# Sliding dilated attention beside a gated FFN: one quadrant run and one Exp for each block's logits, sums of four products everywhere, and a new order of TensorE's work

## The chip, the cores and the metric

The kernel runs on one core of one Trainium2 chip. Its time is device microseconds (us) of one execution; a lower number is better. All runs that are compared were fast (TensorE's clock granted at 0.99 or more of full speed).

## The reference, cut to what matters

```python
def _A_ref(x, wqkv, wo):                 # attention: 32 heads of 16, window 8, dilation 2
    H = 32; Dh = D // H
    W, dil = 8, 2
    qkv = ...(x @ wqkv)...
    idx = pos[:, None] - (jnp.arange(W) * dil)[None, :]
    mask = idx >= 0
    kg = k[:, :, idx_c, :]; vg = v[:, :, idx_c, :]
    logits = jnp.einsum("bhsd,bhswd->bhsw", q, kg) * scale
    attn = _softmax(jnp.where(mask, logits, -1e9), axis=-1)
    o = jnp.einsum("bhsw,bhswd->bhsd", attn, vg)
    return o @ wo                        # s

def _B_ref(x, w_gate, w_up, w_down):     # FFN, 512 -> 1792 -> 512
    h = _gelu(x @ w_gate) * (x @ w_up)
    return h @ w_down                    # y

xn = _layernorm(x)                       # x is 2048 x 512, bf16
return x + _A_ref(xn, ...) * _silu(_B_ref(xn, ...))
```

## The kernel before

The 2048 tokens are worked on in four blocks of 512 (`j` = 0 to 3). For each block TensorE computes QKV; VectorE multiplies q by eight shifted views of k and adds products; TensorE sums what is left over the 16 channels of a head with a "quadrant" matmul, in which 128 rows become 32, so that four of them lie side by side in one PSUM tile (L, the logits); ACT takes the Exp. The window's sums (`sum_ps`), their reciprocals spread back (`b_ps`) and the products with v (`pv`, reduced to O by another quadrant run) follow in the same way. The FFN runs as 14 pairs of g (gate) and u (up) for each block, each four matmuls of 128x512, and y is 14 matmuls for each tile of 128 tokens.

The whole program is a list of tasks. A small list scheduler orders them at build time, by the durations and priorities in the dictionary `G` and by rings of buffers; the instructions are then issued in that fixed order on each engine. `FULL`, `UPACT` and `TRACT` (transposed tiles that ACT copies) say which work is done and by which engine, and `fb`, `ab` and the like are the sizes of the rings; the rest of `G` sets the order and nothing else.

```python
G = dict(
    ... FULL=(2, 3), UPACT=tuple((j, fc) for j in (1, 2, 3) for fc in range(14)),
    BETWEEN={1: 4, 2: 3}, ... fb=4, ab=2, ob=1, prb=6, ...
)
# PSUM: four buffers "f" (qkv, g, u, y, s), two "a" (tr, L, sum, b), one double "O", each 128 x 512 f32

def scores(j, prio):
    full = j in G["FULL"]                       # sums of four products, or of two
    for w2 in range(2):                         # two halves of the window
        ...                                     # 4 products on VectorE, added in pairs; if full, the pairs too
        def reduce(w2=w2, prods=prods):
            L = psa.tile([P, TQ], F32, name="L_ps", tag="a")
            for i in range(1 if full else 2):
                for w4 in range(4):
                    nc.tensor.matmul(L[32 * w4 : 32 * (w4 + 1), :], lhsT=quad[:],
                        rhs=prods[2 * i][:, w4, :], start=(i == 0), stop=(i == 1 or full))
        def expo(w2=w2):
            nc.scalar.activation(out=attn[:, w2, :], in_=tiles["L", j, w2][:], func=AF.Exp)
    ...                                         # sums, recip, spread_back, b_copy
def ffn_pair(j, fc):
    copied_up = (j, fc) in G["UPACT"]           # ACT copies u to SBUF, or VectorE reads it in PSUM
    ...
def out_tile(j, tt, split):
    ...
    if tt == 0:
        s = add_s()
        y = add_y()
    else:
        y = add_y()
        s = add_s()
```

The softmax here doesn't subtract the row's maximum and nothing guards it: scores larger than these inputs give would overflow.

Of the kernel before, what the change touches and what calls it, by code (L numbers as in the profile page):

```python
# [9 lines left out]
ALU = mybir.AluOpType  # L10
# [4 lines left out]
P = 128  # L15
# [10 lines left out]
    MM=0.217, COL8=0.3, COL4=0.2, TR=0.354, PROD=1.167, HMUL=0.582, HMUL2=0.34, STATS=0.881,  # L26
    NORM=0.326, TRCOPY=0.444, ACT1=0.58, ACT2=1.087, TABLE=1.075, HOP=0.136, LOOK=0.275, vst=2.654,
    vload=3.833, vissue=2.706, TRACT=(), x2=13.724, x3=17.04, FULL=(2, 3), UPACT=tuple((j, fc) for j in (1, 2, 3) for fc in range(14)),
    BETWEEN={1: 4, 2: 3}, trig=[0, 0, 3, 3],
    s_prio=[1.0, 2.0, 3.5, 4.0], v_prio=[1.5, 2.0, 3.75, 4.5], e_lat=0.1, b_lat=0.1, p_sum=-1.5,  # L30
    p_red=-0.5, p_tr=-1.0, p_h=-1.4, wo_at=0, wd_at=1, fb=4, ab=2, ob=1, prb=6, vab=2, x_early=[3.2,
    3.5, 3.8, 4.1],
# [5 lines left out]
HMUL = G["HMUL"]  # L38
# [99 lines left out]
def kernel(  # L138
# [23 lines left out]
    def pool(name, bufs, **kw):  # L162
# [9 lines left out]
    prpool = pool("prpool", G["prb"])  # L172
    atpool = pool("atpool", 2)
# [12 lines left out]
        {"xn": 4, "q": 3, "vst": 4, "va": G["vab"], "pr": G["prb"], "attn": 2, "o": 2, "h0": 1, "h1": 1, "gl": 3, "sg": 3,  # L186
# [124 lines left out]
    def layer_norm(j):  # L311
# [38 lines left out]
        def transpose(t, dep, on_act):  # L350
# [17 lines left out]
            a = add("pe", TR, fn, deps=[dep], prio=G["p_tr"], takes=[("a", ("tr", t))], frees=[("xn", t)])  # L368
# [5 lines left out]
        if j == 0:  # L374

            behind = []
            for half in range(2):
                pair = list(ts)[2 * half : 2 * half + 2]
                for t, s in [(t, stat(t, behind)) for t in pair]:
                    transpose(t, norm(t, rstd_act(t, 1, [s])), on_act=t % 2 == 0)  # L380
                behind = [copied[t] for t in pair if t % 2 == 1]
        else:
            for half in range(2):
                pair = list(ts)[2 * half : 2 * half + 2]
                r = rstd_act(pair[0], 2, [stat(t) for t in pair])
                for t in pair:
                    transpose(t, norm(t, r), on_act=(j, half) in G["TRACT"])
# [24 lines left out]
    def qkv(j):  # L412
# [4 lines left out]
        for lo in range(0, TQ, n):  # L417
            for which in range(3):
                for c in range(0, NC, w):
# [47 lines left out]
                    if which == 0 and c == 0 and lo == 0:  # L467
                        takes = [("q", j)]
                    e = add(
                        "act", ACT1, evacuate, deps=[m], prio=-0.5, takes=takes,  # L470
# [45 lines left out]
    def scores(j, prio):  # L516
        exps = []
        full = j in G["FULL"]
        for w2 in range(2):
            prods = []  # L520

            def product(c, w2=w2, prods=prods):
                prod = prpool.tile([P, 4, TQ], BF16, name="prod", tag="pr")
                off = j * TQ + PAD - HALO + 8 * w2
                base = k_sb[:, c, off : off + TQ]
                kwin = bass.AP(
                    tensor=base.tensor, offset=base.offset, ap=[base.ap[0], [2, 4], [1, TQ]]
                )
                nc.vector.tensor_tensor(  # L529
                    out=prod[:],  # L530
                    in0=tiles["q", j][:, c, :].unsqueeze(1).to_broadcast([P, 4, TQ]),
                    in1=kwin,
                    op=ALU.mult,
                )
                prods.append(prod)

            def pair(i, prods=prods):
                a, b = prods[2 * i], prods[2 * i + 1]
                nc.vector.tensor_tensor(out=a[:], in0=a[:], in1=b[:], op=ALU.add)  # L539

            def reduce(w2=w2, prods=prods):
                L = psa.tile([P, TQ], F32, name="L_ps", tag="a")
                tiles["L", j, w2] = L
                for i in range(1 if full else 2):
                    for w4 in range(4):
                        nc.tensor.matmul(  # L546
                            L[32 * w4 : 32 * (w4 + 1), :],
                            lhsT=quad[:],
                            rhs=prods[2 * i][:, w4, :],
                            start=(i == 0),  # L550
                            stop=(i == 1 or full),
                        )

            def expo(w2=w2):
                if w2 == 0:
                    tiles["attn", j] = atpool.tile([P, 2, TQ], BF16, name="attn", tag="attn")
                attn = tiles["attn", j]
                nc.scalar.activation(out=attn[:, w2, :], in_=tiles["L", j, w2][:], func=AF.Exp)

            def masked(w2=w2):  # L560
                a = tiles["attn", j][:, w2, 0:PAD]
                nc.vector.tensor_tensor(out=a, in0=a, in1=mask[:, w2, :], op=ALU.mult)

            ps = []
            key = ("S", j, w2)
            for c in range(NC):
                last = c == NC - 1
                ps.append(
                    add(
                        "dve", PROD, lambda c=c, product=product: product(c),  # L570
                        deps=[q_ready[j], k_ready[j], *ps[-1:]], prio=prio,
                        takes=[("pr", (*key, c))], opens=key,
                        frees=[("q", j)] if w2 == 1 and last else [],
                    )
                )
                if c % 2 == 1:
                    ps.append(
                        add(
                            "dve", PROD, lambda c=c, pair=pair: pair(c // 2), deps=[ps[-1]], prio=prio,
                            opens=key, closes=key if last and not full else None,  # L580
                            frees=[("pr", (*key, c))],
                        )
                    )

            def whole(prods=prods):
                a, b = prods[0], prods[2]
                nc.vector.tensor_tensor(out=a[:], in0=a[:], in1=b[:], op=ALU.add)

            if full:
                ps.append(  # L590
                    add(
                        "dve", PROD, whole, deps=[ps[-1]], prio=prio, opens=key, closes=key,
                        frees=[("pr", (*key, 2))],
                    )
                )
            r = add(
                "pe", G["COL4"] if full else COL8, reduce, deps=[ps[-1]], prio=G["p_red"],
                takes=[("a", ("L", j, w2))], frees=[("pr", (*key, c)) for c in ((0,) if full else (0, 2))],
            )
            e = add(  # L600
                "act", ACT1, expo, deps=[r], prio=-0.6, func="exp",
                takes=[("attn", j)] if w2 == 0 else [], frees=[("a", ("L", j, w2))],
            )
            if j == 0:
                e = add("dve", 0.1, masked, deps=[e], prio=-1.5)
            exps.append(e)
# [41 lines left out]
    def values(j, prio):  # L648
# [10 lines left out]
        for half in range(2):  # L659
            pvs = []  # L660

            def product(g, w2, half=half, pvs=pvs):
                pv = prpool.tile([P, 4, TQ], BF16, name="pv", tag="pr")
                nc.vector.tensor_tensor(  # L664
                    out=pv[:],
                    in0=tiles["attn", j][:, w2, :].unsqueeze(1).to_broadcast([P, 4, TQ]),
                    in1=tiles["va", j, half][:, 4 * (g % 2) : 4 * (g % 2 + 1), 8 * w2 : 8 * w2 + TQ],
                    op=ALU.mult,
                )
                pvs.append(pv)  # L670

            def pair(gg, pvs=pvs):
                a, b = pvs[2 * gg], pvs[2 * gg + 1]
                nc.vector.tensor_tensor(out=a[:], in0=a[:], in1=b[:], op=ALU.add)  # L674

            def reduce(half=half, pvs=pvs):
                o_ps = pso.tile([P, 2, TQ], F32, name="O_ps", tag="o")
                tiles["O", j, half] = o_ps
                for gg in range(2):
                    for e in range(4):  # L680
                        nc.tensor.matmul(  # L681
                            o_ps[32 * e : 32 * (e + 1), gg, :],
                            lhsT=fold4[:, 0, :],
                            rhs=pvs[2 * gg][:, e, :],
# [12 lines left out]
            ps = []  # L697
            key = ("V", j, half)
            for i in range(4):
                last = i == 3  # L700
                ps.append(
                    add(
                        "dve", PROD,
                        lambda i=i, half=half, product=product: product(2 * half + i // 2, i % 2),
                        deps=[n, v_ready[j, half], *ps[-1:]], prio=prio,
                        takes=[("pr", (*key, i))], opens=key,
                        frees=([("va", (j, half))] if last else [])
                        + ([("attn", j)] if last and half == 1 else []),
                    )
                )  # L710
                if i % 2 == 1:
                    ps.append(
                        add(
                            "dve", PROD, lambda i=i, pair=pair: pair(i // 2), deps=[ps[-1]], prio=prio,
# [222 lines left out]
    for j in range(NJ):  # L937
        ffn_pairs(j, NF)
        for tt in range(TPB):
            out_tile(j, tt, j == NJ - 1 and tt == TPB - 1)  # L940
# [31 lines left out]
```

## Time and profile before

| kernel before | |
|---|---|
| time, median of 6 runs | 228.25 us (228.23 to 228.44) |
| span in the profile | 226.5 us |
| TensorE: first QKV matmul, end of the last s | 7.29, 222.85 us |
| quadrant runs for L | 8 (4 of eight matmuls, 4 of four) |
| table loads on ACT | 19 |

The prediction shows the lines themselves and reads them. One word is used throughout: the pitch is the distance between the starts of successive matmuls, 0.216 us for 128x512 here, so a wait of TensorE shows as a start that comes later than the pitch.

### The profile page before, as it was taken

The page shows a single profiled execution, that of the slowest core. Times are in us where ns is not written, and L with a number is a line of the kernel's source. Part 1 is how long each engine was busy: PE and PEld are TensorE (multiplying, and loading weights), DVE is VectorE, ACT ScalarE, POOL GpSimd, SP SyncE. Part 2 cuts the span into 40 slices and gives each one's busy share as a digit, 9 for nine tenths or more (in the row PEclk, how much of TensorE's full clock was granted, in tenths as well). Part 3 has the DMA queues.
Part 4 walks back from the last instruction along what each step waited for, and adds up shares of the span by engine and source line. Part 5 has one row for each costly group of instructions (what it writes and reads, how often), then busy time and mean ns, then how long its engine had stood idle before and what let it go on. Part 6 is the DMA issues. An engine that isn't in the chain of part 4 may idle for free.

```text
span 226.5 us, 3294 instructions
## 1 busy us (share of the span) xinstructions
PE 220.3 (97%) x1230; PEld 106.1 (47%) x1230; DVE 187.9 (83%) x278; ACT 137.4 (61%) x215; POOL 14.8 (7%) x46
## 2 busy tenths in 40 slices
PE   6999999999999999999999999999999999999993
PEld 2897544534544444444444444444444444444462
DVE  4899999999999999899999999999936999322232
ACT  3566675658777346297777435877772187767210
POOL 7100400000022000002100000202000000000000
PEclk9999999999999999999999999999999999999999
DMA  6994990293199500106280010267100100000001
GB/s 205 340 372 155 216 252 4 56 348 110 50 353 273 120 0 23 46 26 143 47 188 0 3 46 26 75 141 163 25 0 26 46 23 0 0 3 0 23 25 46
DMA packets 19216, 22.64 MB, mean 100 GB/s; under 512 B 1392, under 2 KB 18176, under 8 KB 19200
## 3 DMA queue, kind: packets, MB, share of 16 engines
q1 hardware_dynamic: 12832, 11.67, 18.7%
q10 hardware_dynamic: 5056, 6.49, 8.8%
q0 software_dynamic: 1312, 4.28, 8.1%
q8 instruction: 9, 0.15, 0.3%
q14 instruction: 7, 0.06, 0.1%
HBM read 18.22 MB, written 4.21 MB: 99 GB/s over the span
## 4 chain that ended last, share of the span: by engine, by line
PE 95%; DVE 2%; DMA 1%; issue 0%; DVEq 0%
PE y_ps L808 22%; PE g_ps L735 22%; PE u_ps L735 22%; PE qkv_ps L432 19%; PE s_ps L796 6%; PE O_ps L681 2%; PE tr_ps L354 2%; PE L_ps L546 2%; DMA x_sb<-in_A_x_dram 1%; DVE stats L318 1%; PE sum_ps L613 0%; PE b_ps L631 0%; DVE sg L825 0%; DVE xn_t L339 0%; DVE xnT L366 0%
## 5 line engine op out<-in xcount | busy, mean ns | idle before, releaser
L735 PE MATMUL g_ps<-xnT,wg_sb 128*128 128x512 bf16 x224 | 57.5, 379 | 0.0
L735 PE MATMUL u_ps<-xnT,wu_sb 128*128 128x512 bf16 x224 | 57.5, 379 | 0.0
L808 PE MATMUL y_ps<-wd_sb,hT 128*128 128x512 bf16 (+1 forms) x238 | 51.4, 367 | 0.0
L432 PE MATMUL qkv_ps<-xnT,wqkv_sb 128*128 128x512 bf16 (+1 forms) x240 | 43.6, 337 | 0.3 <-DVE xnT L366 0.3
L745 ACT ACTIVATE gl<-g_ps 128x512 bf16<-128x512 f32 x56 | 33.5, 598 | 16.9 <-PE g_ps L735 16.7
L664 DVE TENSOR_TENSOR pv<-attn,v_arr 128x2048 bf16<-128x2048 bf16 x32 | 38.5, 1219 | 0.1
L529 DVE TENSOR_TENSOR prod<-q_sb,k_sb 128x2048 bf16<-128x2048 bf16 x32 | 38.4, 1218 | 0.0
L808 PEld LDWEIGHTS <-hT 128*128 128x128 bf16 x238 | 22.7, 98 | 24.6 <-issue 0.9
L735 PEld LDWEIGHTS <-wu_sb 128*128 128x128 bf16 x224 | 21.5, 98 | 27.1 <-issue 2.1
L735 PEld LDWEIGHTS <-wg_sb 128*128 128x128 bf16 x224 | 21.5, 98 | 26.8 <-issue 1.5
L432 PEld LDWEIGHTS <-wqkv_sb 128*128 128x128 bf16 x240 | 25.0, 108 | 15.9 <-issue 1.8
L820 ACT ACTIVATE sil<-y_ps 128x512 bf16<-128x512 f32 (+1 forms) x17 | 9.7, 572 | 34.8 <-PE y_ps L808 34.8
L758 ACT ACTIVATE hT<-u_ps 128x512 bf16<-128x512 f32 x42 | 25.1, 598 | 8.8 <-PE u_ps L735 8.5
L763 DVE TENSOR_TENSOR hT<-gl,hT 128x512 bf16<-128x512 bf16 x42 | 17.6, 422 | 11.9 <-ACT hT L758 11.8
L825 DVE TENSOR_TENSOR sg<-sil,s_ps 128x512 bf16<-128x512 bf16 (+1 forms) x17 | 11.1, 653 | 12.2 <-PE s_ps L796 8.2
L674 DVE TENSOR_TENSOR pv<-pv 128x2048 bf16<-128x2048 bf16 x16 | 19.5, 1222 | 0.3
L539 DVE TENSOR_TENSOR prod<-prod 128x2048 bf16<-128x2048 bf16 x16 | 19.5, 1222 | 0.3
L504 POOL DMA_DIRECT2D v_arr<-vT_dram x16 | 9.3, 586 | 138.8 <-DVE pv L664 122.9
L796 PE MATMUL s_ps<-wo_sb,o_sb 128*128 128x512 bf16 (+1 forms) x68 | 16.4, 367 | 0.0
L451 ACT ACTIVATE k_sb<-qkv_ps 128x512 bf16<-128x512 f32 x16 | 9.4, 597 | 5.8 <-PE qkv_ps L432 5.8
L318 DVE BATCH_NORM_STATS2 stats<-x_sb 128x6 f32<-128x512 bf16 x16 | 10.8, 675 | 2.3 <-DMA x_sb<-in_A_x_dram 2.3
L445 ACT ACTIVATE q_sb<-qkv_ps 128x512 bf16<-128x512 f32 x16 | 9.5, 597 | 3.4 <-PE qkv_ps L432 3.1
(56 smaller groups left out, 141.2 us busy)
## 6 DMA issues: line engine op xcount, KB each, us to landing
v_arr<-vT_dram SPq DMA_DIRECT2D x16, 260.0 KB, 5.4
v_arr<-vT_dram POOLq DMA_DIRECT2D x16, 260.0 KB, 6.1
vT_dram<-vst SPq DMA_DIRECT2D x16, 128.0 KB, 4.4
out_dram<-sg SPq DMA_DIRECT2D x15, 128.0 KB, 1.7
wg_sb<-in_B_w_gate_dram ACTq DMA_DIRECT2D x2, 896.0 KB, 5.8
wu_sb<-in_B_w_up_dram ACTq DMA_DIRECT2D x2, 896.0 KB, 8.5
wd_sb<-in_B_w_down_dram ACTq DMA_DIRECT2D x1, 1792.0 KB, 9.0
wqkv_sb<-in_A_wqkv_dram SPq DMA_DIRECT2D x2, 512.0 KB, 6.0
```

Source lines behind the costliest of these rows:

```text
L318: nc.vector.bn_stats(out=stats[:, t, :], in_=x_sb[:, t, :])
L432: nc.tensor.matmul(ps[:, i * n : (i + 1) * n], lhsT=wqkv_sb[:, which, ws], rhs=xnT[:, dk, j * TQ + lo : j * TQ + lo + n], start=(dk == 0), ...
L529: nc.vector.tensor_tensor(out=prod[:], in0=tiles["q", j][:, c, :].unsqueeze(1).to_broadcast([P, 4, TQ]), in1=kwin, op=ALU.mult,)
L539: nc.vector.tensor_tensor(out=a[:], in0=a[:], in1=b[:], op=ALU.add)
L664: nc.vector.tensor_tensor(out=pv[:], in0=tiles["attn", j][:, w2, :].unsqueeze(1).to_broadcast([P, 4, TQ]), in1=tiles["va", j, half][:, 4 * ...
L674: nc.vector.tensor_tensor(out=a[:], in0=a[:], in1=b[:], op=ALU.add)
L735: nc.tensor.matmul(ps[:], lhsT=w[:, dk, fc * P : (fc + 1) * P], rhs=xnT[:, dk, j * TQ : (j + 1) * TQ], start=(dk == 0), stop=(dk == NC - 1),)
L745: nc.scalar.activation(out=tiles["gl", j, fc][:], in_=tiles["g_ps", j, fc][:], func=AF.Gelu_apprx_tanh)
L758: nc.scalar.activation(out=hidden(), in_=tiles["u_ps", j, fc][:], func=AF.Copy)
L763: nc.vector.tensor_tensor(out=h, in0=tiles["gl", j, fc][:], in1=u, op=ALU.mult)
L796: nc.tensor.matmul(tiles["s", t, cs.start][:], lhsT=tiles["o", j][:, c, tt * P : (tt + 1) * P], rhs=wo_sb[:, c, cs], start=(c == 0), stop= ...
L808: nc.tensor.matmul(tiles["y", t, cs.start][:], lhsT=tiles["h", j, fc // (NF // 2)][:, fc % (NF // 2), tt * P : (tt + 1) * P], rhs=wd_sb[:, ...
```

## The change

Its intent: make L in one run of eight matmuls on a double PSUM tile, with one 1024-wide Exp, where there were two runs and two Exps. To keep that run at eight matmuls in every block, VectorE adds four products everywhere (`FULL`), which costs it work in blocks 0 and 1. For that it is relieved elsewhere: ACT copies u in block 0 too, and eight transposed tiles. Six pairs stand between the QKV of blocks 1 and 2 (before: four there, and three between blocks 2 and 3), and y of a block's first two tiles goes by halves of h, with s after y.

```diff
 G = dict(
-    ... FULL=(2, 3), UPACT=tuple((j, fc) for j in (1, 2, 3) for fc in range(14)),
-    BETWEEN={1: 4, 2: 3}, trig=[0, 0, 3, 3], ...  wd_at=1, fb=4, ab=2, ob=1, prb=6, ...
+    ... FULL=(0, 1, 2, 3), BETWEEN={1: 6}, TRACT=((2, 0), (2, 1), (3, 0), (3, 1)),
+    trig=[0, 6, 1, 3], ... smode=[2, 2, 2, 2], ... wd_at=2, fb=4, ab=2, ob=1, prb=3, rsb=4, ...
 )
 ...
-            def reduce(w2=w2, prods=prods):
-                L = psa.tile([P, TQ], F32, name="L_ps", tag="a")
-                tiles["L", j, w2] = L
-                for i in range(1 if full else 2):
+        def reduce():
+            L = pso.tile([P, 2, TQ], F32, name="L_ps", tag="o")
+            tiles["L", j] = L
+            for w2 in range(2):
+                for i in range(per):
                     for w4 in range(4):
                         nc.tensor.matmul(
-                            L[32 * w4 : 32 * (w4 + 1), :],
+                            L[32 * w4 : 32 * (w4 + 1), w2, :],
                             lhsT=quad[:],
-                            rhs=prods[2 * i][:, w4, :],
+                            rhs=results[per * w2 + i][:, w4, :],
                             ...
-            def expo(w2=w2):
-                ...
-                nc.scalar.activation(out=attn[:, w2, :], in_=tiles["L", j, w2][:], func=AF.Exp)
+        def expo():
+            tiles["attn", j] = atpool.tile([P, 2, TQ], BF16, name="attn", tag="attn")
+            nc.scalar.activation(out=tiles["attn", j][:], in_=tiles["L", j][:], func=AF.Exp)
 ...
-            h = tiles["h", j, fc // (NF // 2)][:, fc % (NF // 2), :] if copied_up else hidden()
-            u = h if copied_up else tiles["u_ps", j, fc][:]
-            nc.vector.tensor_tensor(out=h, in0=tiles["gl", j, fc][:], in1=u, op=ALU.mult)
+            h = tiles["h", j, fc // (NF // 2)][:, fc % (NF // 2), :]
+            nc.vector.tensor_tensor(out=h, in0=tiles["gl", j, fc][:], in1=h, op=ALU.mult)
 ...
-        if tt == 0:
-            s = add_s()
-            y = add_y()
+            elif tt < 2 and mode == 2:
+                if tt == 0:
+                    add_y((0,))
+                    parts[1][0]((0,))
+                y = add_y((1,))
+                s = add_s()
```

Cut from this diff: the scheduler's other durations and priorities, new rings for sums (`res`) apart from products, and modes of the y order that are not used here (0: s of the first tile before y; 3: y of a whole tile at once).

## The prediction

> **What bounds the kernel now.** I read the page's first part, then the chain, then TensorE's timeline, and only then the other engines.
>
> ```profile
> PE 220.3 (97%) x1230; PEld 106.1 (47%) x1230; DVE 187.9 (83%) x278; ACT 137.4 (61%) x215; POOL 14.8 (7%) x46
> PE   6999999999999999999999999999999999999993
> PE 95%; DVE 2%; DMA 1%; issue 0%; DVEq 0%
> PE y_ps L808 22%; PE g_ps L735 22%; PE u_ps L735 22%; PE qkv_ps L432 19%; PE s_ps L796 6%; PE O_ps L681 2%; PE tr_ps L354 2%; PE L_ps L546 2%; DMA x_sb<-in_A_x_dram 1%; DVE stats L318 1%; PE sum_ps L613 0%; PE b_ps L631 0%; DVE sg L825 0%; DVE xn_t L339 0%; DVE xnT L366 0%
> ```
>
> TensorE is busy in all slices but the first and last, and 95% of the chain that ended last is matmuls. From the first QKV matmul (7.29 us) to the last s (221.81 + 1.04 = 222.85) it makes one stream of 215.56 us. Ahead of it stand 7.29 us of loads and layer norm, behind it 3.65 us of the last gate and store, to 226.5; the timed run is 1.75 us above the span. A busy share can hide overlap in the records (a matmul record is 379 ns long), so I checked the stream by its pitch. In the timeline (start, length, engine, line, operation, count), runs of four 128x512 matmuls start 0.864 us apart, 0.216 each:
>
> ```profile
> 36.44 1.03 PE L735 MATMUL g_ps<-xnT,wg_sb 128*128 128x512 bf16 x4
> 37.30 1.03 PE L735 MATMUL u_ps<-xnT,wu_sb 128*128 128x512 bf16 x4
> 38.26 0.62 PE L546 MATMUL L_ps<-prod,quad 128*32 128x512 bf16 x8
> 38.80 7.96 PE L432 MATMUL qkv_ps<-xnT,wqkv_sb 128*128 128x512 bf16 x36
> 46.70 0.61 PE L546 MATMUL L_ps<-prod,quad 128*32 128x512 bf16 x8
> 47.24 2.76 PE L432 MATMUL qkv_ps<-xnT,wqkv_sb 128*128 128x512 bf16 x12
> ...
> 95.87 1.03 PE L796 MATMUL s_ps<-wo_sb,o_sb 128*128 128x512 bf16 x4
> 96.82 0.40 PE L546 MATMUL L_ps<-prod,quad 128*32 128x512 bf16 x4
> 97.15 1.04 PE L735 MATMUL g_ps<-xnT,wg_sb 128*128 128x512 bf16 x4
> ```
>
> What an L run adds to the stream is the distance between its neighbours' starts less the neighbour's own matmuls. Eight matmuls: 38.80 - 37.30 - 0.86 = 0.64, and 47.24 - 38.80 - 36 x 0.216 = 0.67; mean 0.65. Four: 97.15 - 95.87 - 0.86 = 0.42. So a round of four column quadrants costs 0.22 (they run side by side) and every run 0.2 more for entering and leaving it. With these pitches (256 wide 0.109, a transpose 0.055, an O run 0.66, a sum run 0.33, b 0.22), the order of before laid end to end gives 222.8 us for its end, against 222.85 measured: **TensorE has no stall to remove. Only fewer matmuls, or fewer runs of the quadrant shape, shorten it.**
>
> The windows by stage show the only neighbour that could take over the bound:
>
> ```profile
> 31.30:80.90 49.60, 49.60 (x266) 22.20 (x265) 48.49 (x53) 34.10 (x51) 2.32 (x4) 1.00 0.57 163
> 97.20:139.60 42.40, 42.40 (x224) 18.33 (x221) 41.37 (x52) 27.39 (x42) 2.32 (x4) 1.00 0.27 64
> 139.60:181.60 42.00, 42.00 (x217) 18.36 (x216) 35.75 (x48) 26.88 (x42) 2.33 (x4) 1.00 0.27 64
> 181.60:222.85 41.25, 41.24 (x219) 19.77 (x217) 19.30 (x31) 23.65 (x37) 0.00 (x0) 1.00 0.04 13
> ```
>
> The columns are the stretch, its length, then busy time (and count) of PE, PEld, DVE, ACT, POOL. VectorE is 98% busy until 139.6, then falls to 47%. ACT has a third of its time free.
>
> **What the Trainium skill says.** "TensorEngine Tiling (Array Packing)", Key Properties, says that changing the tiling mode drains the TensorE: the trace agrees, the 0.2 us on each quadrant run. "TensorE: Matmul & The Clock Gate", section "Wait — 56ns, not 53.3ns?", gives 215.7 ns start to start for 512 columns warm; the trace has 216. "VectorE: DVE Perf Modes", the perf-mode tier table, gives tensor_tensor 2x for bf16 in SBUF and 1x with PSUM; the trace has 682 ns for the h product that reads PSUM and 422 ns for the one from SBUF. "ScalarE: Activation LUTs", What ACT_TABLE_LOAD costs, states 1283 ns and a drain of 1380 ns; the trace has the 1283, but no drain: a load at 38.11 is followed by the Exp at 39.41.
>
> **The change part by part.**
>
> TensorE. L was 2 runs of 8 in each of blocks 0 and 1, and 2 runs of 4 in each of blocks 2 and 3. It becomes one run of 8 in every block (48 matmuls become 32; the built program's order agrees). Saved: 2 x 0.65 in blocks 0 and 1, 2 x (0.42 + 0.42 - 0.65) = 0.38 in blocks 2 and 3: **1.7 us, all on the path that sets the end.** Everything else on TensorE (QKV, pairs, y, s, O, sum, b) has the same counts and only another order; one more break between transposes costs some 0.02.
>
> VectorE. One sum of two sums more in each half of blocks 0 and 1: +4 x 1.22 = 4.9. The 14 h products of block 0 read SBUF: 14 x (0.422 - 0.682) = -3.6. Eight transposed tiles are copied by ACT: -8 x 0.413 = -3.3. Sum -2.0, to about 186.
>
> ACT. 14 copies of u at 0.598 = +8.4; 8 transposes at 0.594 = +4.8; Exp 4 x 1.02 (as the 1024-wide o_sb copy) for 8 x 0.597 = -0.7; table loads 19 become 15: -5.1. Sum +7.4, to 145 us. These lie beside matmuls.
>
> Orders. The six pairs now all stand between QKV of block 1 and of block 2, and y of two tiles by halves of h puts 14 matmuls ahead of the first that needs the last h, and s after y. They remove no work; they move deadlines.
>
> So I laid the new order of TensorE end to end with the same pitches (it ends at 221.1) and asked at each point where VectorE feeds it whether VectorE is there. Its pitches are from its timeline: a 2048 operation 1.135 us behind an independent one; 3.53 for two products and their sum; an h product 0.34; gate and residual 1.06; stats 0.82; rec and two norms 0.83; recip and cast 1.2.
>
> - L of block 0: TensorE is there at 45.9. VectorE: the norms delay the first product to 25.7; then 14 operations (16.6), one pair of norms (0.7) and six h (2.0), less a few tenths of drain that the h fill: done at 44.7. About 1.0 to spare.
> - L of block 1: TensorE at 63.5. From 44.7: 16.6, recip, mask and cast 1.3, normalise 0.6: 63.1. **Some 0.2 to spare after the hop: the tightest point.**
> - O of block 0: TensorE at 73.3 and 82.2, VectorE at 72.0 and 80.6.
> - L of block 2: 104.9 against 103.4; O of block 1: 115.6 and 124.5 against 113.9 and 122.5; L of block 3: 147.2 against 145.5.
> - s of the first tile: o_sb lands 1.75 after its O run starts, s comes 0.66 + 7 x 0.216 = 2.17 after: 0.4 to spare.
>
> A block in the middle asks VectorE for 26 x 1.14 + 14 x 0.34 + 4 x 1.06 + 1.9 = 40.5 us in 42.3 of TensorE, so the lead grows. In the first 31 us the transposes wait on norms with 0.2 to 1 to spare.
>
> Small losses: in blocks 2 and 3 the Exp now falls between pairs, so ACT spends 2 x 1.28 + 1.02 = 3.6 us away from four PSUM buffers that TensorE fills in 4 x 0.86 = 3.5. I allow 0.1 for each, and 0.1 for the tight L of block 1.
>
> **Sum:** 228.25 - 1.7 + 0.15 (part of these losses will not occur) = **226.7 us**, 0.7% faster.
>
> **The rivals.**
> 1. VectorE becomes the bound early. It carries blocks 0 and 1's added sums (4.9 us) where it is 98% busy, against 3.6 saved there on h and 3.3 on copies. Against: the sums balance and every deadline above holds. For: leads of 0.2 to 1 us, which a late x or v transfer could eat. If L of block 1 came 1 us late, TensorE would stand once by that: 227.5; late at several points, 228 to 230.
> 2. ACT becomes the wait: from 19 to 32 us it has 12 evacuations and 8 transposes, some 11 us in 12, and in the pairs two evacuations per 1.73 us plus two table loads. If the ring of four PSUM buffers runs dry by 1 us in the head and in blocks 2 and 3: 228 to 229.
> 3. A transfer: wd is now issued after QKV of block 3, near 64, needed at 79.2. It took 9.0 us to land, so it is there at 73; the second loads of wg and wu have more. If wd took 6 us longer: 227 and up. I hold it hidden.
> 4. The order alone gains more, beyond the matmuls. The stream of before has no stall, the head and tail code stay as they are, so I see no way to lose more than 1.8.
>
> **Range and chances.** The floor is 228.25 - 1.8 = 226.4, less 0.2 for what the pitches miss; upward one or two of the rivals may cost about 1 us: 226.2 to 228.2. Faster by 2% needs 223.7, below the floor: 0.01. Slower by 2% needs over 6 us of stalls against leads that are met: 0.02. Within 2%: 0.97.
>
> **What would show it right or wrong.** Right: L in 32 matmuls and four runs of some 0.65 each; TensorE's stream starts at 7.3 and ends near 221.2; o_sb, h and table loads in the counts above; VectorE near 186 and ACT near 145 us. Wrong: TensorE idle behind res (rival 1), behind free buffers with Exp or gelu as the releaser (rival 2), or behind wd at 79 (rival 3); a stream that starts later than 7.3; or an L run dearer than 0.65 because it now reaches over two PSUM banks.

## The result, and the profile after

The kernel after takes **227.08 us** (median of 6 runs, 227.05 to 227.25). The ratio to before is 0.9948, with a 95% interval of 0.9936 to 0.9961: 0.5% faster. A ratio here is the mean time of one kernel's fast runs over the mean of the other's of the same rounds, so it is not quite the ratio of the medians. The prediction said 226.7 in a range of 226.2 to 228.2, so it held. The gain was 1.17 us where it said 1.55.

The page of the kernel after begins with the engines' busy time; the second line here is the chain that ended last, by engine.

```profile
PE 218.9 (97%) x1214; PEld 106.0 (47%) x1214; DVE 186.0 (83%) x273; ACT 142.6 (63%) x229; POOL 14.9 (7%) x46
PE 90%; ACT 4%; DVE 2%; DMA 1%; issue 1%; DVEq 0%
```

Sixteen matmuls are gone from TensorE, as they should be. But the chain is no longer matmuls alone: 4% of it is now ACT, which wasn't on the chain of before. TensorE's timeline of the kernel after (start, length, engine, line, operation, tiles, shapes, count) shows both the gain and where a part of it went.

```profile
41.62 4.48 PE L434 MATMUL qkv_ps<-xnT,wqkv_sb 128*128 128x512 bf16 x20
46.02 0.61 PE L599 MATMUL L_ps<-res,quad 128*32 128x512 bf16 x8
46.57 4.51 PE L434 MATMUL qkv_ps<-xnT,wqkv_sb 128*128 128x512 bf16 x20
...
104.06 1.03 PE L741 MATMUL g_ps<-xnT,wg_sb 128*128 128x512 bf16 x4
105.01 0.61 PE L599 MATMUL L_ps<-res,quad 128*32 128x512 bf16 x8
105.56 1.04 PE L741 MATMUL u_ps<-xnT,wu_sb 128*128 128x512 bf16 x4
...
109.12 0.29 PE L632 MATMUL sum_ps<-attn,fold 128*32 128x128 bf16 x8
109.35 1.04 PE L741 MATMUL u_ps<-xnT,wu_sb 128*128 128x512 bf16 x4
110.50 1.02 PE L741 MATMUL g_ps<-xnT,wg_sb 128*128 128x512 bf16 x4
...
151.85 1.04 PE L741 MATMUL u_ps<-xnT,wu_sb 128*128 128x512 bf16 x4
153.00 1.02 PE L741 MATMUL g_ps<-xnT,wg_sb 128*128 128x512 bf16 x4
```

The L run of block 0 adds 46.57 - 41.62 - 20 x 0.216 = 0.63 us to the stream, that of block 2 adds 105.56 - 104.06 - 0.864 = 0.64, and the other two the same. Four runs cost 2.55; the eight of before cost 2 x 2 x 0.65 + 4 x 0.42 = 4.28. So **1.73 us were saved**. The last lines show the loss: from u at 109.35 to g are 1.15 us where 0.864 is the pitch, so TensorE waited 0.29. The same stands in the pairs of the next block: 153.00 - 151.85 - 0.864 = 0.29. Apart from the quadrant runs, the sums and their like, which add the same as before, no other stretch of the timeline leaves the pitch. 1.73 - 0.57 = 1.16 is the whole of the result: the stream starts at 7.29 as before and ends at 221.65, 1.20 earlier, and the tail behind it is 3.65 us as before.

What ended that wait is seen on ACT's timeline of the kernel after, in the same stretch; the brackets give the idle time before an instruction and who ended it.

```profile
105.12 0.60 ACT L751 ACTIVATE gl<-g_ps 128x512 bf16<-128x512 f32 x1 [0.27 <-PE g_ps L741]
105.73 1.28 ACT L609 ACT_TABLE_LOAD   x1
107.03 1.02 ACT L609 ACTIVATE attn<-L_ps 128x1024 bf16<-128x1024 f32 x1
107.95 0.59 ACT L762 ACTIVATE hT<-u_ps 128x512 bf16<-128x512 f32 x1
108.56 1.28 ACT L751 ACT_TABLE_LOAD   x1
109.85 0.60 ACT L751 ACTIVATE gl<-g_ps 128x512 bf16<-128x512 f32 x1
```

Number the pairs from 0. The g at 110.50 is that of pair 8. The four PSUM buffers go round in the order g6, u6, g7, u7, g8, so g8 takes the buffer of g6. TensorE wrote g6 at 106.44, but ACT reads it only at 109.85: ahead of it stand a table load for the Exp, the Exp, one copy of u and the table load back to gelu. That gelu ends at 110.45 and g8 starts at 110.50.

One window of the kernel after (stretch, length, busy time and count of PE, PEld, DVE, ACT, POOL; the last three columns are TensorE's clock, the share of the DMA engines and GB/s) answers to the first of those in the prediction.

```profile
31.20:80.00 48.80, 48.80 (x262) 22.38 (x260) 48.46 (x55) 38.62 (x63) 2.19 (x4) 1.00 0.54 150
```

VectorE is as full there as it was, 48.46 of 48.80 us, and TensorE has no gap. ACT took on the work: 38.62 us, 79% of the stretch, where it had 34.10 in 49.60, 69%.

### The profile page after: what moved, and what is told of

It reads as the page before. It is cut to its first block, busy times and chain, and to the rows that moved or that the text cites. A ratio compares the mean times of both kernels' runs of the same rounds, so it can differ in the third digit from the quotient of the medians.

```text
span 225.3 us, 3262 instructions
## 1 busy us (share of the span) xinstructions
PE 218.9 (97%) x1214; PEld 106.0 (47%) x1214; DVE 186.0 (83%) x273; ACT 142.6 (63%) x229; POOL 14.9 (7%) x46
## 3 DMA queue, kind: packets, MB, share of 16 engines
q0 software_dynamic: 1312, 4.28, 8.2%
## 4 chain that ended last, share of the span: by engine, by line
PE 90%; ACT 4%; DVE 2%; DMA 1%; issue 1%; DVEq 0%
PE y_ps L803 22%; PE g_ps L741 20%; PE u_ps L741 19%; PE qkv_ps L434 19%; PE s_ps L791 6%; PE O_ps L708 2%; PE tr_ps L354 2%; ACT L751 1%; DMA x_sb<-in_A_x_dram 1%; ACT gl L751 1%; ACT attn L609 1%; ACT L609 1%; DVE stats L318 1%; PE L_ps L599 0%; DVE xn_t L339 0%
## 5 line engine op out<-in xcount | busy, mean ns | idle before, releaser
L762 ACT ACTIVATE hT<-u_ps 128x512 bf16<-128x512 f32 x56 | 33.5, 598 | 10.1 <-PE u_ps L741 9.9
L546 DVE TENSOR_TENSOR res<-prod 128x2048 bf16<-128x2048 bf16 x32 | 39.1, 1221 | 0.6
L686 DVE TENSOR_TENSOR prod<-attn,v_arr 128x2048 bf16<-128x2048 bf16 x32 | 38.7, 1219 | 0.0
L766 DVE TENSOR_TENSOR hT<-gl,hT 128x512 bf16<-128x512 bf16 x56 | 23.5, 421 | 12.0 <-ACT hT L762 11.8
L719 ACT ACTIVATE o_sb<-O_ps 128x1024 bf16<-128x1024 f32 x8 | 8.2, 1023 | 9.0 <-PE O_ps L708 9.0
L458 ACT ACTIVATE vst<-qkv_ps 128x512 bf16<-128x512 f32 x16 | 9.0, 602 | 3.7 <-PE qkv_ps L434 2.1
```

Source lines behind the costliest of these rows:

```text
L546: nc.vector.tensor_tensor(out=res[:], in0=a[:], in1=b[:], op=ALU.add)
L686: nc.vector.tensor_tensor(out=prod[:], in0=tiles["attn", j][:, w2, :].unsqueeze(1).to_broadcast([P, 4, TQ]), in1=tiles["va", j, half][:, 4 ...
L762: nc.scalar.activation(out=hidden(), in_=tiles["u_ps", j, fc][:], func=AF.Copy)
L766: nc.vector.tensor_tensor(out=h, in0=tiles["gl", j, fc][:], in1=h, op=ALU.mult)
```

## The experiments

Each was run against the kernel before on the same chip; all gave right results. The time of the kernel after for comparison is 227.08.

| run | median us (range) | ratio to before (95%) | against after |
|---|---|---|---|
| e1 direct u5 | 227.56 (227.45 to 227.63) | 0.9966 (0.9953 to 0.9978) | +0.48 |
| e9 sum with O | 227.09 (227.07 to 227.10) | 0.9945 (0.9932 to 0.9959) | +0.01 |
| e10 both | 226.63 (226.44 to 226.80) | 0.9925 (0.9912 to 0.9937) | -0.45 |
| e11 fifth bank | 226.61 (226.49 to 228.31) | 0.9942 (0.9921 to 0.9963) | -0.47 |
| e12 fifth and join | 225.86 (225.83 to 225.87) | 0.9894 (0.9880 to 0.9909) | -1.22 |
| e2 two runs | 228.84 (228.78 to 229.21) | 1.0026 (1.0013 to 1.0038) | +1.76 |
| e3 two Exps | 228.19 (228.18 to 228.44) | 1.0001 (0.9987 to 1.0014) | +1.11 |
| e4 sums of two | 229.39 (228.86 to 229.50) | 1.0043 (1.0030 to 1.0057) | +2.31 |
| e5 u from PSUM | 228.63 (228.47 to 228.83) | 1.0015 (1.0002 to 1.0029) | +1.55 |
| e6 y whole | 228.67 (228.61 to 228.82) | 1.0018 (1.0005 to 1.0030) | +1.59 |
| e7 s first | 229.10 (229.09 to 229.30) | 1.0035 (1.0020 to 1.0050) | +2.02 |
| e8 between | 228.83 (228.73 to 231.28) | 1.0055 (0.9998 to 1.0112) | +1.75 |

The medians of before in these rounds were 228.25 to 228.44. A fifth run of e4 took 237.29 at a clock of 0.986; it is slow and left out, of the median too. The last column compares medians of different rounds and chips, so a tenth or two of it can be noise.

**The theory** after the result: the change saves 1.73 us of quadrant runs and loses 0.57 to the window in which ACT is away for the Exp. Its rival: the 0.57 is lost to something else (hops between engines, VectorE), and would come back elsewhere if that window were opened.

### e11: one more PSUM buffer, for one g

```diff
-            ps = psf.tile([P, TQ], F32, name=name, tag="f")
+            if name == "g_ps" and (j, fc) in ((1, 8), (2, 8)):
+                ps = psa.tile([P, TQ], F32, name=name, tag="a")
+            else:
+                ps = psf.tile([P, TQ], F32, name=name, tag="f")
```

> The changed kernel in the same order on every engine; only g of pair 8 in blocks 1 and 2 is written to one of the two banks that the head's transposes used and that stand free there, so the pairs have five banks at that point. No engine's work changes. Theory A (the waits of 0.29 us are for the bank that gelu of pair 6 gives back behind Exp and two table loads): both go, TensorE's stream ends 0.57 earlier, 226.5 us. Rival B (something else holds TensorE there): 227.1. Reading u from PSUM made it 227.6, because that bank came back still later, behind recip.

TensorE's timeline of this kernel, at the place of the wait:

```profile
109.35 1.04 PE L744 MATMUL u_ps<-xnT,wu_sb 128*128 128x512 bf16 x4
110.23 1.03 PE L744 MATMUL g_ps<-xnT,wg_sb 128*128 128x512 bf16 x4
```

The order of every engine is untouched and only the buffer differs; g now follows u by 0.88. The wait is gone in both blocks and nothing takes its place: the last s starts at 220.06, 0.55 earlier than in the kernel after, and the profiled run took 226.51. That is what the saving alone would give, 228.25 - 1.73 = 226.52. This shows the cause of the 0.57. The median is 226.61; two of the six runs were higher (227.23 and 228.31), and they pull the ratio up. Why they were higher stays open.

### e1: VectorE reads the one u of the window in PSUM

```diff
+        direct = (j, fc) in ((1, 5), (2, 5))
         def evacuate():
-            nc.scalar.activation(out=hidden(), in_=tiles["u_ps", j, fc][:], func=AF.Copy)
+            h = hidden()
+            if not direct:
+                nc.scalar.activation(out=h, in_=tiles["u_ps", j, fc][:], func=AF.Copy)
         def mult():
-            nc.vector.tensor_tensor(out=h, in0=tiles["gl", j, fc][:], in1=h, op=ALU.mult)
+            u = tiles["u_ps", j, fc][:] if direct else h
+            nc.vector.tensor_tensor(out=h, in0=tiles["gl", j, fc][:], in1=u, op=ALU.mult)
```

> The changed kernel in the same order, but u of pair 5 in blocks 1 and 2 (the pair around the L run) isn't copied by ACT; VectorE multiplies it out of PSUM. Theory A (the 0.5 us that the prediction missed are the two waits of 0.29 us in TensorE behind Exp and its two table loads, while the four PSUM buffers run full): ACT comes back 0.5 us earlier, both waits go, TensorE's stream ends 0.57 earlier: 226.5 us. Rival B (the missed time is in the L runs themselves, now over two banks, or in VectorE): unchanged, 227.1.

It came out at 227.56, which neither theory had: a miss. TensorE's timeline of this kernel, and under it VectorE's:

```profile
110.13 1.02 PE L741 MATMUL u_ps<-xnT,wu_sb 128*128 128x512 bf16 x4 [0.60 <-ACT gl L751]
```

```profile
109.58 0.96 DVE L642 RECIPROCAL rs<-sum_ps 128x128 f32<-128x128 f32 x1 [0.62 <-PE sum_ps L632]
...
110.72 0.68 DVE L771 TENSOR_TENSOR hT<-gl,u_ps 128x512 bf16<-128x512 bf16 x1
```

The copy left ACT, but its work went to an engine that is in order too: VectorE's product with u5 stands behind the reciprocal, and that behind the sum, which needs the Exp. So u5's buffer comes back at 111.4 and not at 108.5, and u of pair 7 waits 0.68 for the next one, which the gelu of pair 6 gives back. The wait did not go; it moved one matmul group ahead and grew (in the next block it is 0.16). It does say that the window, not a hop, decides.

### e9: the sums share a quadrant run with O

```diff
+            both, waits, after_sum = later[j + 1] if half == 0 and j + 1 < NJ else (None, [], None)
+            def run(reduce=reduce, both=both):
+                if both is not None:
+                    both()               # the sums of the next block
+                reduce()                 # O of this block, first half
-            r = add("pe", COL8, reduce, deps=[(chain[-1], G["o_lat"])], ...)
+            r = add("pe", COL8 + (0.12 if both else 0.0), run, deps=[(chain[-1], G["o_lat"]), *waits], ...)
```

> The softmax sum of blocks 1, 2, 3 is put directly ahead of the first O run of the block before, so that two quadrant runs stand side by side and enter the shape once. If the 0.2 us is the price of entering and leaving the shape, each joined sum costs 0.11 instead of 0.33 on TensorE. Theory A: in blocks 2 and 3 the 0.33 us that leave the pairs behind Exp only turn into a longer wait for ACT there (0.29 becomes 0.62), so just block 1 gains: 227.0. Rival B (the wait behind Exp isn't a fixed window of ACT): three gains of 0.22, 226.4.

```profile
108.83 1.03 PE L759 MATMUL u_ps<-xnT,wu_sb 128*128 128x512 bf16 x4
110.31 1.02 PE L759 MATMUL g_ps<-xnT,wg_sb 128*128 128x512 bf16 x4 [0.45 <-ACT gl L769]
```

The time did not move (227.09). TensorE's timeline shows why: without the sum run, TensorE reaches g8 a third of a microsecond earlier, and the wait is 110.31 - 108.83 - 0.864 = 0.62 where it was 0.29. The end of the window is fixed by ACT; what TensorE saves inside it is waited away. The join also saved 0.21 in block 1, ahead of both windows; that is lost again because the sum now adds 0.12 to each O run behind the two windows. That is the theory's reading, and against the rival.

### e10: e9, and u of pairs 5 and 6 read in PSUM

```diff
+        direct = (j, fc) in ((1, 5), (2, 5), (1, 6), (2, 6))   # on top of e9
```

> Sum joined with O, and u of pairs 5 and 6 of blocks 1 and 2 read from PSUM by VectorE. Theory A: both gains arrive, 227.1 - 0.57 - 0.66 = 225.9, some 0.1 to 0.2 of waits left: 226.0. Rival: as in the two parts alone.

226.63, with waits of 0.13 and 0.48 left, the second on a buffer that VectorE gives back. Better than the change, and worse than expected for the reason of e1.

### e12: e9 and e11 together

Its edit is the two diffs of e9 and e11.

> The fifth bank and the sums joined to O. With the ring no longer the limit, the three joined sums should now each be worth 0.22: 226.5 - 0.66 = 225.9 us. If the joined sums stay worth nothing: 226.5.

It took **225.86 us**, as expected: 1.06% faster than before by the ratio of the means and 1.22 us faster than the change, the best of all. TensorE's timeline of this kernel where sum and O lie side by side:

```profile
112.25 1.03 PE L762 MATMUL u_ps<-xnT,wu_sb 128*128 128x512 bf16 x4
113.21 0.30 PE L632 MATMUL sum_ps<-attn,fold 128*32 128x128 bf16 x8
113.33 0.60 PE L716 MATMUL O_ps<-res,fold 128*32 128x512 bf16 x8
113.87 1.04 PE L762 MATMUL g_ps<-xnT,wg_sb 128*128 128x512 bf16 x4
```

Both runs together add 113.87 - 112.25 - 0.864 = 0.76; apart they add 0.33 + 0.65 = 0.98. With the window open, the three joints pay: 3 x 0.22 = 0.66, and the last s starts 0.67 earlier than in e11 (219.39 against 220.06).

### e2: two L runs, one Exp

```diff
-        def reduce():
-            L = pso.tile([P, 2, TQ], F32, name="L_ps", tag="o")
-            for w2 in range(2):
+        def reduce(w2):                  # one task for each half, its own quadrant run
+            if w2 == 0:
+                tiles["L", j] = pso.tile([P, 2, TQ], F32, name="L_ps", tag="o")
```

> The changed kernel with L again in two PE runs of four per block, into the two halves of the same tile, still with one Exp of 1024 and sums of four everywhere. By the prediction's own term each block loses 2 x 0.42 - 0.65 = 0.19, in sum 0.77: 227.85 us, with the waits behind Exp as they are. If one run were worth nothing beyond its matmuls: 227.1.

It cost 1.76 where 0.77 was expected: a miss. The runs themselves cost 0.88 (eight add 3.43 us, 0.43 each, where the four add 2.55). TensorE's timeline of this kernel has the rest:

```profile
109.15 0.30 PE L635 MATMUL sum_ps<-attn,fold 128*32 128x128 bf16 x8
110.27 1.02 PE L744 MATMUL g_ps<-xnT,wg_sb 128*128 128x512 bf16 x4 [0.81 <-ACT gl L754]
```

The scheduler put the second L run behind a u and not behind a g. The group right after L is then the g whose gelu stands behind the Exp (in the kernel after, a u comes between), so TensorE wants its buffer one group of 0.86 sooner: waits of 0.90 and 0.52 in the two blocks, for 0.29 each. (The stream also began 0.2 later in this profile.) One position in the order cost 0.85 here, about as much as the extra runs.

### e3: two L runs, two Exps of 512

```diff
-            L = pso.tile([P, 2, TQ], F32, name="L_ps", tag="o")
+            L = psa.tile([P, TQ], F32, name="L_ps", tag="a")          # one tile for each half
-            nc.scalar.activation(out=tiles["attn", j][:], in_=tiles["L", j][:], func=AF.Exp)
+            nc.scalar.activation(out=tiles["attn", j][:, w2, :], in_=tiles["L", j, w2][:], func=AF.Exp)
```

> L in two runs and two Exps of 512 per block, into two one-bank tiles as before the change; 21 table loads instead of 15; sums of four everywhere. Theory A: the runs cost +0.77 as in the other experiment, but ACT is away from the pairs only 2 x 1.28 + 0.6 = 3.2 us at a time, less than the 3.5 us that four buffers hold, so the two waits of 0.29 go: 227.1 + 0.8 - 0.5 = 227.4. Rival (fewer table loads and one long Exp gain time by themselves): 228.0 or more.

228.19, 0.8 over what was expected: a miss. The two waits of 0.29 are gone, as the theory said of a shorter Exp in the window. But the first Exp of block 0 now falls among the pairs, and there is a new wait of 0.41 there (TensorE's timeline of this kernel):

```profile
39.48 1.03 PE L745 MATMUL u_ps<-xnT,wu_sb 128*128 128x512 bf16 x4
40.75 1.02 PE L745 MATMUL g_ps<-xnT,wg_sb 128*128 128x512 bf16 x4 [0.24 <-ACT gl L755]
```

The runs cost 0.87 and the tail 0.28 more (3.93), all of it behind the issue of the last store. Together 0.87 - 0.57 + 0.41 + 0.28 = 0.99 of the 1.11; the rest I could not place.

### e4: sums of two products in blocks 0 and 1

```diff
-    FULL=(0, 1, 2, 3)
+    FULL=(2, 3)
```

> Blocks 0 and 1 with sums of two products again, but in one PE run of 16 matmuls per block; the rest as changed. VectorE loses four operations (4.9 us), TensorE gains 16 matmuls = two more rounds of 0.216 in each of two blocks: +0.86 on TensorE's stream, 227.9. If VectorE were the bound in the first 80 us: 227.1 or less.

It came out 1.5 over what was expected: a miss. TensorE's timeline of this kernel, at the first y:

```profile
80.24 1.03 PE L741 MATMUL u_ps<-xnT,wu_sb 128*128 128x512 bf16 x4
81.69 1.69 PE L803 MATMUL y_ps<-wd_sb,hT 128*128 128x512 bf16 x7 [0.42 <-DMA wd_sb<-in_B_w_down_dram]
```

The longer L runs cost what they should: sixteen matmuls add 0.43 more in each of two blocks, 0.86. The waits make the larger part: 0.59 for wd, 0.31 for an evacuation, and 0.48 twice behind the Exp (for 0.29 twice). The evacuation stands behind four issues of the wo load on ACT's queue, 2.6 us. In sum 0.86 + 0.59 + 0.31 + 0.96 - 0.57 = 2.15 of the 2.31. The wait for wd is the third rival of the prediction come true: wd took 15.6 us to land where it took 8.0 in the kernel after. With less to do, VectorE gives the buffers of v back sooner, and eight loads of `v_arr` are issued from 65.4 to 74 beside wd (issued at 66.0); in the kernel after the first of them come at 70.2, and wd has nearly landed. That these loads slowed wd is likely, but no run isolates it.

### e5: u of block 0 read in PSUM

```diff
+        direct = j == 0                  # mult and evacuate as in e1
```

> Same order, but all 14 h products of block 0 read u from PSUM on VectorE (0.68 for 0.42 us) and ACT doesn't copy. ACT loses 8.4 us of work. By the leads of the trace of the changed kernel (res of block 1 is complete at 62.9, its L run starts at 63.65) six slower products (1.6 us) make L of block 1 some 0.9 to 1.0 late, and the second O run of block 0 by 0.2: 228.2. Rival (ACT is what TensorE waits for in block 0): no slower than 227.1.

```profile
63.92 0.40 PE L599 MATMUL L_ps<-res,quad 128*32 128x512 bf16 x4
64.82 0.40 PE L599 MATMUL L_ps<-res,quad 128*32 128x512 bf16 x4 [0.50 <-DVE res L546]
```

It came out 0.4 over what was expected. TensorE's timeline of this kernel shows the L run of block 1 broken in two, 0.57 late for VectorE's second sum (with the second entry into the shape the stream loses 0.67), which is the first rival of the prediction come true. A g at 71.21 waits 0.54 for a buffer that VectorE gives back, and a y 0.29. The relief in block 0 is needed.

### e6 and e7: y of whole tiles, s after y or before

```diff
-    smode=[2, 2, 2, 2]
+    smode=[3, 3, 3, 3]    # e6: y of a whole tile, then its s
+    smode=[0, 0, 0, 0]    # e7: as before: s of the first tile, then its y
```

> y of two tiles by halves undone in the way that keeps s behind y (y of 14 matmuls, then s, tile by tile). The second half of the first y comes 1.5 us after the last u instead of 3 (and 0.66 for O): h of pair 13 is there 1.3 us after it, so 0 to 0.3 per block is lost: 227.1 to 227.6. If y by halves carries more, a wait of TensorE on hT before L803's second half shows it.

> s of the first tile ahead of its y, as in the kernel before, the rest as changed. In block 0 the second O run is due directly after the last u (79.2) but its last sum is complete at 80.1, and s needs o_sb 1.75 us after the O run starts: 0.9 + 1.3 = some 2.2 us of waiting in block 0; in the later blocks 0 to 0.5. 229.3 us. If the place of s doesn't matter: 227.1.

TensorE's timeline of e6, block 0:

```profile
82.39 0.61 PE L708 MATMUL O_ps<-res,fold 128*32 128x512 bf16 x8
82.94 0.61 PE L791 MATMUL s_ps<-wo_sb,o_sb 128*128 128x512 bf16 x2
84.14 0.61 PE L791 MATMUL s_ps<-wo_sb,o_sb 128*128 128x512 bf16 x2 [0.59 <-ACT o_sb L719]
```

e6 missed. I had y wait for the last h; what waits is s, 0.77 for the copy of O (`o_sb`) on ACT, because O falls right before it. A u at 99.01 waits 0.19. And L of block 2 moves behind a u, so the wait behind that Exp becomes 0.67, as in e2. In e7, as expected in size but not in its parts (0.9 and 1.3 were expected in block 0), O waits 0.54 for VectorE, s 0.76 for `o_sb`, and the Exp window takes 0.67 and 0.30. In block 0 the halves of h therefore pay by what they put between O and s.

### e8: the pairs between QKV blocks split as before

```diff
-    BETWEEN={1: 6}
+    BETWEEN={1: 4, 2: 3}
```

> Four pairs between QKV of blocks 1 and 2 and three between 2 and 3, as before, the rest as changed. TensorE's work is the same, ACT has two more table loads where it has room: 227.1 to 227.5. If the six pairs in one place carry the gain: 228 or more, with TensorE waiting for res of block 0 or 1.

228.83; one of its runs took 231.28 at a clock of 0.993, which makes its interval wide. TensorE waits 1.60 us once, and not for VectorE. ACT's timeline of this kernel (ACTq is its queue issuing loads):

```profile
45.27 2.60 ACTq L906 DMA_DIRECT2D wo_sb<-in_A_wo_dram  x4
...
49.20 1.02 ACT L609 ACTIVATE attn<-L_ps 128x1024 bf16<-128x1024 f32 x1
50.12 2.06 ACT L458 ACTIVATE vst<-qkv_ps 128x512 bf16<-128x512 f32 x4
```

The four issues of the wo load, a table load of 1.28 and the Exp stand in a row: from the end of a copy of k at 45.87 to 50.12 ACT evacuates nothing, and the first g after that QKV waits for the first of the four copies of v (it ends near 50.7; g starts at 50.76). The kernel after splits these issues to either side of evacuations. The mechanism is the same as at pair 8, with a longer absence.

## Why the prediction was right, and which term was off

- **The bound.** "Only fewer matmuls, or fewer runs of the quadrant shape, shorten it": right. The stream's own work fell by 1.73 for 1.7 predicted; laid end to end the order was to end at 221.1, and 221.65 less the 0.57 of waits is 221.08. And e12 gained again by the same rule, with three fewer entries into the shape. The fear that a run over two PSUM buffers is dearer was unfounded: 0.63 to 0.64.
- **VectorE and its deadlines.** Right. Its time is 186.0 (predicted 186). `res` of block 0 is complete at 44.5 and TensorE there at 46.02 (44.7 and 45.9 predicted). The tightest point was met too: the last sum of block 1 ends at 62.92 and L starts at 63.65 (63.1 and 63.5). e5 shows that the relief for it was no decoration. One reading was loose, and nothing rests on it: between the 98% and the 47% lies a stage, 139.6 to 181.6, with VectorE 85% busy (35.75 of 42.00 us).
- **ACT.** Counts right, sum too high: 142.6 for 145. I added mean durations, but neighbouring ACT records overlap. After the window of block 2, for one, three ACT instructions of 0.60 each start 0.50 and 0.47 apart, so in a dense stretch each costs less busy time than its length.
- **The Exp window: the mis-sized term.** The step read "I allow 0.1 for each", and with the 0.1 for L of block 1 I then booked 0.15 in all. Measured: 0.29 for each, 0.57, and nothing at L of block 1. The working compared 3.6 us of ACT's absence with 3.5 of TensorE's filling. It left out two instructions of the same queue: the copy of u between the Exp and the second table load, and the gelu itself, at whose end the buffer is free. From the first load (105.73) to that end (110.45) are 4.7 us. e11 settles that this wait is the whole of the difference, e9 that its end is fixed by ACT. The prediction also named the blocks by their attention, 2 and 3; the waits are in the pairs of blocks 1 and 2, where those Exps fall. It is its second rival at half the size it was given there, and in the pairs alone: in the head, which that rival also named, nothing waited.
- **Transfers.** Right for the change: wd was issued at 63.8, landed 8.0 us later and was needed at 79.2, so some 7 us were spare. e4 shows how that can go: its wd took 15.6 us.
- **What the prediction did not ask** is what each part is worth. Undone alone, e2 to e8, each part costs 1.1 to 2.3 us, in sum far above the 1.17 that all gain together. Before had no stall with the old parts in the old order; that suggests, but does not show, that most parts gain nothing themselves and only keep the one-run L from causing waits in its own order. In these runs I could place each loss to within some 0.15 us, once the last store is counted, which took 0.2 to 0.3 us longer in the profiles of e3, e4, e6 and e7 (for e7 0.65 + 0.76 + 0.67 + 0.30 - 0.57 + 0.30 = 2.11 for 2.02; 0.65 is the late O run with its second entry into the shape). Not undone alone, and so of unknown worth, are the eight transposed tiles on ACT, the new rings, and the new times of the weight loads.

## What to carry to other kernels

When TensorE has no gaps, count how often it enters another tiling shape, and put runs of the same shape side by side: the size of that gain can be read off the pitch, and it arrives where no wait behind it takes it back (0.22 for each joint in e12, nothing in e9). Then lay each absence of the evacuating engine (table loads, a wide Exp, load issues) against the PSUM buffers TensorE fills meanwhile, and count everything in that queue up to the end of the instruction that frees the buffer. Here a free buffer of another pool for one tile was a better cure (e11, 226.61) than handing the work to a second engine that is in order itself (e1, 227.56).

## What the Trainium skill lacked or had wrong

- "TensorEngine Tiling (Array Packing)", Key Properties, names the drain on a change of mode but gives no figure. Here: 0.2 us for each run, in and out, and 0.76 instead of 0.98 us for the sum and O runs side by side, which share it (e12). That the 0.2 is all drain is not shown.
- "ScalarE: Activation LUTs", What ACT_TABLE_LOAD costs: the 1283 ns of the load are seen, but not its drain of 1380 ns. A load that starts at 105.73 is followed by the Exp at 107.03, so a switch costs 1.3 us here, half of what the page's sum gives.
- I found no page that says for this chip how long issuing loads on ACT's queue holds back ACT's own instructions ("DMA: Bandwidth & Descriptors" has a cost per issue only in a comparison for trn3): four issues took 2.60 us, and TensorE waited 1.60 us behind them and the Exp (e8).
